# One scale per pair of input tiles, weight sums written in place, and a table for attention's pace, in a two-branch kernel

## The chip, the cores and the metric

The kernel runs on one core of a Trainium2 chip. The core's engines work side by side, each through its own instructions in order: TensorE (PE; its weight loads are shown apart as PEld), VectorE (DVE), ScalarE (ACT), GpSimd (POOL) and SyncE (SP, which here only issues DMAs). The metric is the device time of one execution in microseconds (us). The time before is 1770.59 us, the median of three runs (1760.23 to 1774.22).

## The reference

Two independent computations share one output, side by side along the last axis:

```python
# branch A: attention of 32 heads of width 32 over a sliding window of 256 keys
q, k, v = split(x @ wqkv)                      # x: 2048 x 1024
scores = q @ k.T * 32 ** -0.5, masked to 0 <= i - j < 256
a = (softmax(scores) @ v) @ wo
# branch B: a Fourier layer written with four matrices
p0 = xb @ dft_hid_re.T ; p1 = xb @ dft_hid_im.T    # 2048 x 1024
b = dft_seq_re @ p0 - dft_seq_im @ p1
out = concatenate([a, b], axis=-1)             # 2048 x 2048, float32
```

All inputs are float32. Branch A's inputs are larger by a factor of 8 than the usual draw, so its softmax is sharp and its products need more than half precision.

## The kernel before

**Products.** A float32 matrix is divided by a power of two taken from its largest entry, and split into a high and a low float16 part (`split`: ACT writes the high part, DVE the low part); a product is then three float16 passes (high-high, high-low, low-high). The largest entry is found by `top` (a DVE reduction of one tile to a column), `spread` (over the tiles), and `scale_of` (a small transposing matmul on PE, and four or five small DVE instructions). The large products of branch B and the last one of A are done in two-by-two blocks with seven multiplications in place of eight (`seven`), for which sums of blocks are made beforehand.

**Order of the work.** PE's order is written out. First come 96 *order steps* of one 128x512 product each (24 large matmuls): the q, k and v projections. Then come 48 *units* in four *rounds* of twelve, 84 large matmuls each: four units of branch B's first product (kind x: pairs of tiles of `xb` times the hidden weights, `p1_`), then eight of its second (kind c: rows of the sequence matrix, `p2_`). Rounds are numbered by p (real, imaginary part) and c (left, right half); the first round stores its result plainly, the others add to the output through an accumulating DMA of POOL (`store`). Eight last products with `wo` follow (`po`).

**Attention in between.** Attention has 256 blocks (a group of two heads by 128 queries). It is a Python generator; `tick(n)` is called after every 8 (steps) or 4 (units) large matmuls, adds `n * rate[0]` to an account, and takes one half-block from the generator for each whole number. A block's chain: PE makes scores (`s`, `far`), DVE masks them and finds maxima (`mx`), ACT exponentiates and writes the high half, DVE the low half (`hl`), SP transposes by DMA (`t<-hl`), POOL masks two copies (`z`, `t`), and six blocks later (`LAG`) PE multiplies by v (`pv<-vt`). Before, the pace is one number times a share: 0.6 in steps, 1 in units, 0.2 in a round's fourth unit. That is 0.88 blocks a step and 5.11 a unit.

**Preparation in the steps.** `at(n, f)` hangs work on step n. `scan(key, k, n, step)` loads k tiles one after the other from step n and reduces each one step later. Before: `wd1` (imaginary hidden weights) from step 9, `B` (all sixteen tiles of `xb`, for one scale) from 22, `wd0` from 40, `wo` from 73. `xp(m, n)` makes the sums of the m-th pair of `xb` tiles, eight pairs from step 41, four steps apart, and stores them to DRAM (`xs`); `wp(p, k, n)` makes the sums of the hidden weights. Both use one buffer, `wx`, for their float32 raws (`praw`) and results (`pout`). The hidden weights' seven sums live in seven slots: four in `reg2`, three in `wx`. For p = 0 the first four were written into their slots, the last three went to DRAM and came back at step 91; for p = 1 all seven go to DRAM and are loaded in the second round (`w_slot`).

**Other queues.** Without an explicit constraint, the framework's scheduler decides where in an engine's queue an instruction lands, SP's above all.

Of the kernel before, what the change touches and what calls it, by code (L numbers as in the profile page):

```python
# [53 lines left out]
def fused_kernel(ctx: ExitStack, tc: tile.TileContext, xa, wqk, wv, wo, xb, wd, cs, out):  # L54
# [7 lines left out]
    wds = [tc.dram_tile((7, P, 2, 4, CH), F16, name=f"wds{p}") for p in range(2)]  # L62
# [116 lines left out]
    vB4 = const.tile([P, 1], F32, name="vB4")  # L179
# [200 lines left out]
    def at(n, f, *args):  # L380
# [100 lines left out]
    def scan_load(key, i):  # L481
        if key == "B":
            src, shape = xb[i], [ND, P]
        elif key == "wo":
# [12 lines left out]
    def scan_scale(key):  # L497
        if key == "B":
            scale_of(key, vB[:, 0:1], vB[:, 1:2])
            nc.vector.tensor_scalar(vB4, vB[:, 1:2], 0.25, None, op0=ALU.mult)  # L500
        elif key[:2] == "wd":
# [9 lines left out]
    def fa_known():  # L511
        for p in range(2):
# [38 lines left out]
    def scan(key, k, n, step):  # L551
        for i in range(k):
            at(n + step * i, scan_load, key, i)
            at(n + step * i + 1, scan_top, key, i, k)
        at(n + step * (k - 1) + 3, scan_scale, key)
# [29 lines left out]
    def xp_step(n, m, step):  # L585
        r1, r2 = (praw(m % 2 * 2 + j).rearrange("p (d t) -> p d t", t=P) for j in range(2))

        def made(at_, src):
# [3 lines left out]
                  src, vB4, behind_act)  # L592
            keep(n + 1, xs[m][:, at_:at_ + 2 * w], t)

        if step == 0:
            made(0, r1)
        elif step == 1:
# [3 lines left out]
        elif step == 2:  # L601
# [6 lines left out]
    def wp_load(p, k):  # L608
        for b in range(4):
            nc.sync.dma_start(praw(b), wd[p, 1 - b % 2, 2 * (b // 2) + k].rearrange("p d c -> p (d c)"))  # L610

    def wp_step(n, p, k, step):
        b1, b2, b3, b4 = (praw(b).rearrange("p (d c) -> p d c", c=CH) for b in range(4))

        def fill(pos, raw):
            if p == 0 and pos < 4:
                t = reg2o[:, pos, :, 2 * k:2 * k + 2]
            else:
                t = pout().rearrange("p (h d c) -> p h d c", h=2, c=CH)
                keep(n + 1, wds[p][pos, :, :, 2 * k:2 * k + 2], t)  # L620
# [38 lines left out]
    def w_slot(p, pos):  # L659
# [520 lines left out]
```

## Time and profile before

The profiled execution took 1775.21 us, 1773.5 of them between the first and the last instruction (the span).

| | us |
|---|---|
| median of the runs | 1770.59 |
| profiled execution | 1775.21 |
| its span | 1773.5 |
| steps 0 to 39 (and the start) | 236.0 |
| steps 40 to 71 | 183.9 |
| steps 72 to 95 | 141.2 |
| units 0 to 11 (round one) | 256.7 |
| units 12 to 23 (round two) | 275.9 |
| units 24 to 35 (round three) | 281.2 |
| units 36 to 47 (round four) | 248.6 |
| the last products | 150.0 |

How to read it: a row of the windows view has a stretch and its length, then busy time of PE, PEld, DVE, ACT and POOL, each with its instructions in brackets, then the granted share of the TensorE clock, the mean busy share of the sixteen DMA engines, and GB/s. A row of waits has who waited for whom: us in total, times, the longest. A row of groups has line, engine, operation, out<-in, shapes, count, then busy us, mean ns of one, then the idle time before them and what ended it. Rows in order of time have start and length.

### The profile page before, as it was taken

Reading aid. Unit: us, or ns where it says so; the run is one execution under the profiler, and the core shown is the slowest. Engines: PE = TensorE matmul, PEld = TensorE weight load, DVE = VectorE, ACT = ScalarE, POOL = GpSimd, SP = SyncE. Lnnn points to the kernel's source line nnn. Section 1 sums busy time; section 2 is a strip of 40 time slices with the busy share of each in tenths; the row PEclk is TensorE's granted clock in tenths of the full one; section 3 lists DMA queues with packets and bytes.
Section 4 is the critical chain, followed back from the end, with each engine's and each line's share of the span. In section 5 each row is a group of like instructions: output and inputs, shape, how many; then the busy total and the mean of one; then the engine's idle time right before and its main releaser. Section 6 shows DMA issues by size and latency. Waiting matters only on the chain.

```text
span 1773.5 us, 30898 instructions
## 1 busy us (share of the span) xinstructions
PE 1710.9 (96%) x10980; PEld 854.1 (48%) x10980; DVE 1381.1 (78%) x2365; ACT 1116.0 (63%) x1939; POOL 431.5 (24%) x698
## 2 busy tenths in 40 slices
PE   9999999999999999999999989999898998999998
PEld 4444454545545545555544544545444444444443
DVE  7878987888894899985998866899686697586542
ACT  3335565665564888886878866888685686463322
POOL 0000221322132223332333423325243323100000
PEclk9999999999999999999999999999999999999999
DMA  9649999999999849999999999959989966854431
GB/s 344 199 158 281 323 283 300 286 270 310 270 253 259 198 100 210 213 209 237 194 282 172 207 163 229 206 115 186 186 171 204 205 144 105 231 99 95 131 95 72
DMA packets 473084, 363.32 MB, mean 205 GB/s; under 512 B 377440, under 2 KB 410208, under 8 KB 471648
## 3 DMA queue, kind: packets, MB, share of 16 engines
q1 hardware_dynamic: 466016, 336.17, 76.2%
q0 software_dynamic: 6912, 25.17, 8.9%
q8 instruction: 86, 1.41, 0.3%
q14 instruction: 70, 0.57, 0.1%
HBM read 178.52 MB, written 109.31 MB: 162 GB/s over the span
## 4 chain that ended last, share of the span: by engine, by line
PE 59%; DVE 18%; DMA 12%; ACT 5%; issue 4%; SPq 1%; POOL 1%; DVEq 0%; ACTq 0%; POOLq 0%
PE p_a L113 15%; PE pv L113 9%; PE p_b L113 7%; DMA t<-hl 7%; PE pq L113 7%; PE pk L113 6%; PE po_a L113 5%; PE p_c L113 4%; PE po_b L113 2%; PE s L113 2%; DVE hl L253 2%; DVE mx L239 2%; DVE reg L795 2%; DVE raw_u L752 1%; DVE y L996 1%
## 5 line engine op out<-in xcount | busy, mean ns | idle before, releaser
L249 ACT ACTIVATE s<-s,bias,escs 128x256 f32<-128x256 f32 (+1 forms) x512 | 270.1, 528 | 11.7
L253 DVE TENSOR_TENSOR hl<-s,hl 128x512 f16<-128x512 f32 (+1 forms) x256 | 170.6, 667 | 92.6 <-ACT hl L252 91.8
L113 PE MATMUL p_a<-reg,un_c 128*128 128x512 f16 x960 | 229.5, 381 | 7.7 <-ACT y L994 7.6
L267 POOL TENSOR_SCALAR_AFFINE_SELECT z<-t 128x512 f16<-128x512 f16 x224 | 171.9, 770 | 248.6 <-PE pv L113 128.2
L242 ACT ACTIVATE bias<-mx,pshift,escs 128x2 f32<-128x2 f32 x256 | 98.3, 384 | 168.2 <-DVE mx L239 165.7
L113 PEld LDWEIGHTS <-reg 128*128 128x128 f16 x1344 | 129.4, 98 | 143.0 <-issue 3.0
L246 POOL TENSOR_SCALAR mark<-bias 128x1 f32<-128x1 f32 x128 | 50.9, 398 | 570.3 <-ACT bias L242 547.3
L252 ACT ACTIVATE hl<-s 128x512 f16<-128x512 f32 (+1 forms) x256 | 148.8, 581 | 55.2 <-DMA t<-hl 49.8
L269 POOL TENSOR_SCALAR_AFFINE_SELECT t<-t 128x512 f16<-128x512 f16 x224 | 174.3, 783 | 12.4
L113 PE MATMUL pk<-reg,wu_k 128*128 128x512 f16 x768 | 174.6, 381 | 2.7 <-DVE wu_k L120 2.7
L113 PEld LDWEIGHTS <-un_b 128*128 128x128 f16 x1152 | 110.0, 98 | 132.7 <-issue 12.6
L239 DVE TENSOR_REDUCE mx<-s 128x2 f32<-128x512 f32 (+1 forms) x256 | 171.0, 668 | 2.9
L113 PE MATMUL pv<-reg,reg 128*128 128x512 f16 x768 | 171.9, 379 | 0.0
L113 PEld LDWEIGHTS <-un_c 128*128 128x128 f16 x1152 | 110.0, 98 | 127.3 <-issue 12.3
L113 PEld LDWEIGHTS <-un_a 128*128 128x128 f16 x1152 | 110.2, 98 | 121.5 <-issue 7.1
L113 PE MATMUL pq<-reg,wu_q 128*128 128x512 f16 x672 | 150.0, 379 | 3.8 <-DVE yq L120 2.9
L113 PE MATMUL p_b<-reg,un_b 128*128 128x512 f16 x576 | 139.7, 382 | 11.9 <-DVE reg L795 4.9
L113 PE MATMUL p_a<-reg,un_a 128*128 128x512 f16 x576 | 138.4, 382 | 3.4 <-DVE y L996 3.4
L113 PE MATMUL p_c<-reg,un_a 128*128 128x512 f16 x576 | 136.5, 379 | 0.0
L113 PEld LDWEIGHTS <-qk 96*128 96x128 f16 x1056 | 88.3, 98 | 79.8 <-issue 10.6
L237 DVE COPY_PREDICATED s<-upper,far 128x256 f32<-128x256 uint32 x224 | 94.4, 421 | 35.7 <-PE s L113 35.4
L113 PEld LDWEIGHTS <-wu_k 128*128 128x128 f16 x768 | 74.5, 98 | 85.4 <-DVE wu_k L120 3.2
(196 smaller groups left out, 3076.4 us busy)
## 6 DMA issues: line engine op xcount, KB each, us to landing
raw_u<-in_cs_dram SPq DMA_DIRECT2D x64, 512.0 KB, 4.9
qk<-qk SPq DMA_DIRECT2D x64, 384.0 KB, 5.3
out_dram<-y POOLq DMA_DIRECT2D x36, 512.0 KB, 8.0
qk<-yq SPq DMA_DIRECT2D x96, 128.0 KB, 4.2
qk<-yk SPq DMA_DIRECT2D x96, 128.0 KB, 3.7
xs<-wx SPq DMA_DIRECT2D x24, 512.0 KB, 5.0
wds<-wx SPq DMA_DIRECT2D x20, 512.0 KB, 5.7
vs<-yv SPq DMA_DIRECT2D x32, 264.0 KB, 4.4
```

Of the source, the lines that this page charges most:

```text
L113: fixed[:] = [nc.tensor.matmul(*args, **kwargs)]
L237: nc.vector.copy_predicated(s[:, :, P:], upper2, d["far"] if nb == 3 else never2)
L239: nc.vector.tensor_reduce(mx, sv, axis=AX.X, op=ALU.max, negate=True)
L242: nc.scalar.activation(bias, mx, AF.Identity, bias=pshift, scale=es)
L246: marks[:] = [nc.gpsimd.tensor_scalar(mark, bias[:, 0:1], 1.0, None, op0=ALU.mult)]
L249: nc.scalar.activation(sv[:, h], sv[:, h], AF.Exp, bias=bias[:, h:h + 1], scale=es)
L252: nc.scalar.activation(hi, sv, AF.Copy)
L253: behind[:] = [nc.vector.tensor_tensor(lo, sv, hi, op=ALU.subtract)]
L267: nc.gpsimd.affine_select(out=z, in_=pk, compare_op=ALU.is_gt, fill=0.0, base=0, pattern=[[0, 4], [-1, P]], channel_multiplier=1)
L269: nc.gpsimd.affine_select(out=pk, in_=pk, compare_op=ALU.is_ge, fill=0.0, base=0, pattern=[[0, 4], [1, P]], channel_multiplier=-1)
L752: nc.vector.tensor_tensor(o, a, b, op=op)
L795: nc.vector.tensor_tensor(lo, src, hi, op=ALU.subtract)
```

## The change

Three things change.

1. *A scale per pair.* The scan `B` goes. Each `xp(m)` loads its pair a step earlier, reduces its two tiles (`top_xp`), and takes a scale of its own (`vxp`), so it runs over six steps in place of four. Part one's eviction multiplies by a column that evens the pairs' scales (`fx`). `wo` is now scanned at steps 20 to 38, `wd0` from 42.
2. *Part-one sums in place.* For p = 0 the raws of the hidden weights come into the rotating pool of five (`load_raw`) in place of `wx`, and all seven sums are written into their slots; the stores and loads between go. For p = 1 the seven loads are hung on other turns of the second round. `w_finish` of the q and k weights runs three steps ahead of their use, not two.
3. *Pace.* A table in blocks per unit, for the x units (`FIRST`) and c units (`SECOND`) of each round; the rest is spread over steps 24 to 95 by `EARLY`.

```diff
-    wds = [tc.dram_tile((7, P, 2, 4, CH), F16, name=f"wds{p}") for p in range(2)]
+    wds = tc.dram_tile((7, P, 2, 4, CH), F16, name="wds")
...
-    SHARE = {"p": 0.6, "x": (1.0, 1.0, 1.0, 0.2), "c": 1.0}
-    base = 2.0 * (NG * NCH * 2 * QB + 2 * LAG) / (
-        24 * (len(order) - START) * SHARE["p"] + 84 * (4 * sum(SHARE["x"]) + (24 + LAST - 0.7) * SHARE["c"]))
-    rate = [base * SHARE["p"]]
+    FIRST = ((7.2, 5.2, 4.9, 0.6), (5.2, 5.2, 4.9, 0.6), (3.3, 5.2, 4.9, 0.6), (3.3, 5.2, 4.9, 0.6))
+    SECOND = ((2.4, 5.0, 5.0, 5.0, 5.0, 5.0, 5.0, 7.0), (2.2, 4.6, 4.6, 4.6, 4.6, 3.9, 3.9, 4.2),
+              (2.4, 4.6, 4.6, 4.6, 4.6, 5.0, 5.0, 4.2), (2.4, 4.6, 4.6, 4.6))
+    EARLY = {n: (0.9, 1.05, 1.05, 1.0, 0.95, 1.05)[(n - START) // 12] for n in range(START, len(order))}
+    in_units = sum(sum(a) for a in FIRST + SECOND) - 0.7 * SECOND[3][LAST - 1]
+    early = (NG * NCH * 2 * QB + LAG - in_units) / sum(EARLY.values())
+    rate = [0.0]
...
     def fa_known():
+        nc.vector.tensor_reduce(vB[:, 0:1], vxp[:, 0], axis=AX.X, op=ALU.max)
+        nc.vector.reciprocal(vB[:, 1:2], vB[:, 0:1])
+        nc.vector.tensor_scalar(fx, vxp[:, 0], vB[:, 1:2], 4.0 * DOWN, op0=ALU.mult, op1=ALU.mult)
...
-            at(n - 2, w_finish, kd, g)
+            at(n - 3, w_finish, kd, g)
...
     scan("wd1", 8, 9, 1)
-    scan("B", 16, 22, 1)
-    scan("wd0", 8, 40, 4)
-    scan("wo", 8, 73, 2)
-    at(72, fa_known)
+    scan("wo", 8, 20, 2.5)
+    scan("wd0", 8, 42, 3.5)
+    at(75, fa_known)
...
         if step == 0:
+            for j, r in enumerate((r1, r2)):
+                top(f"xp{m}", r, j, 2)
+            spread(f"xp{m}", 2)
+        elif step == 1:
+            scale_of(f"xp{m}", vxp[:, 0, m:m + 1], vxp[:, 1, m:m + 1])
+            nc.vector.tensor_scalar(vxp[:, 1, m:m + 1], vxp[:, 1, m:m + 1], 0.25, None, op0=ALU.mult)
             made(0, r1)
...
-            nc.sync.dma_start(praw(b), wd[p, 1 - b % 2, 2 * (b // 2) + k].rearrange("p d c -> p (d c)"))
+            src = wd[p, 1 - b % 2, 2 * (b // 2) + k]
+            if p == 1:
+                nc.sync.dma_start(praw(b), src.rearrange("p d c -> p (d c)"))
+            else:
+                held[k, b] = load_raw(src, [2, CH], f"wd{k}_{b}")
...
-            if p == 0 and pos < 4:
-                t = reg2o[:, pos, :, 2 * k:2 * k + 2]
+            if p == 0:
+                t = slot(pos)[:, :, 2 * k:2 * k + 2]
...
-        at(n - 1, xp_load, m)
-        for step in range(4):
-            at(n + step, xp_step, n + step, m, step)
+        at(n - 2, xp_load, m)
+        for i, step in enumerate((0, 2, 3, 4, 5)):
+            at(n - 1 + step, xp_step, n - 1 + step, m, i)
...
-    for pos in range(4, 7):
-        at(91, w_slot, 0, pos)
...
+            rate[0] = 2 * early * EARLY.get(n, 0.85) / 24
...
-                for pos in range(7):
-                    do(c0 + pos, 2, w_slot, 1, pos)
+                for pos, (j, turn) in enumerate(((0, 1), (0, 4), (4, 2), (5, 2), (5, 5), (6, 2), (6, 5))):
+                    do(c0 + j, turn, w_slot, pos)
...
-            rate[0] = base * (SHARE["x"][i] if kind == "x" else SHARE["c"])
+            rate[0] = 2 * ((FIRST if kind == "x" else SECOND)[2 * p + c] + (0,) * 8)[i] / 84
...
-                seven(f"p1_{n}", i, uns.pop(n), slot, y1, y2, 4.0 * DOWN, lambda t, y: None, x_hook)
+                seven(f"p1_{n}", i, uns.pop(n), slot, y1, y2, fx[:, 4 * c + i:4 * c + i + 1],
+                      lambda t, y: None, x_hook)
```

Where the pace puts the blocks, counted in PE's order (blocks begun when the step or unit begins):

| | step 40 | step 72 | step 96, unit 0 | unit 12 | unit 24 | unit 36 |
|---|---|---|---|---|---|---|
| before | 15 | 43 | 64 | 121 | 178 | 236 |
| changed | 17 | 54 | 81 | 138 | 187 | 236 |

DVE's order around the second pair of `xb` tiles, near step 46. Here `wx` holds the pair's raws and results, `yk` is an evicted projection, `s`, `mx` and `hl` belong to attention blocks. Before:

```order
L237 COPY_PREDICATED s_2570<-upper,far 128x2x128
L752 TENSOR_TENSOR wx<-wx 128x512
L239 TENSOR_REDUCE mx_2576<-s_2570 128x2
L752 TENSOR_TENSOR wx<-wx 128x512
L120 SCALAR_TENSOR_TENSOR yk_1_2606<-pk_1_2561,kf,yk_1_2606 128x512
L120 SCALAR_TENSOR_TENSOR wx<-wx,vB_105 128x512
L237 COPY_PREDICATED s_2626<-upper,far 128x2x128
```

The same engine and place in the changed kernel:

```order
L120 SCALAR_TENSOR_TENSOR yk_3_2593<-pk_3_2545,kf,yk_3_2593 128x512
L120 TENSOR_REDUCE top_xp_2606<-wx 128x1 x2
L120 SCALAR_TENSOR_TENSOR wx<-wx,vxp 128x1024
L238 COPY_PREDICATED s_2621<-upper,far 128x2x128
L317 TENSOR_TENSOR ohl_0_3_2525<-o_0_3_2367,ohl_0_3_2525 128x256
L254 TENSOR_TENSOR hl_2568<-s_2554,hl_2568 128x512
L120 TENSOR_REDUCE top_xp_2609<-top_xp_2606 128x1
L240 TENSOR_REDUCE mx_2627<-s_2621 128x2
L120 SCALAR_TENSOR_TENSOR yk_0_2694<-pk_0_2612,kf,yk_0_2694 128x512
```

The pair's two reductions (`top_xp`, both in one row) and the small instructions of its scale now stand among the evictions and score maxima of these steps, and read the tile that a DMA has just filled.

SP's order at the start of the second round's c units, with the seven loads of the imaginary weights' sums (`<-wds`), the sequence matrix's tiles (`raw_u`) and attention's transposes. Before:

```order
L660 DMA reg_85<-wds_62 128x4096 x3
L255 DMA_TRANSPOSE t_10620<-hl_10617 128x8x128
L660 DMA reg_85<-wds_62 128x4096
L318 DMA_TRANSPOSE ot_0_0_10717<-ohl_0_0_10714 128x4x128
L660 DMA wx<-wds_62 128x4096
L105 DMA raw_u_0_10812<-in_cs_dram 128x1024
L205 DMA qk_0_3_10852<-qk 96x2048
L660 DMA wx<-wds_62 128x4096
L105 DMA raw_u_1_10933<-in_cs_dram 128x1024
L337 DMA ots<-ot_0_0_10717 128x512
L660 DMA wx<-wds_62 128x4096
```

The same queue and place in the changed kernel:

```order
L671 DMA reg_84<-wds 128x4096
L319 DMA_TRANSPOSE ot_1_0_11254<-ohl_1_0_11251 128x4x128
L671 DMA reg_84<-wds 128x4096
L256 DMA_TRANSPOSE t_11299<-hl_11296 128x8x128
L338 DMA ots<-ot_1_0_11254 128x512
L671 DMA reg_84<-wds 128x4096 x2
L671 DMA wx<-wds 128x4096 x2
L105 DMA raw_u_0_11440<-in_cs_dram 128x1024
L105 DMA raw_u_1_11557<-in_cs_dram 128x1024
L671 DMA wx<-wds 128x4096
```

The seven loads stand together at the head of the c units in both; the turns on which the code hangs them reach over seven units.

More of the change, by code (lines that the diff above doesn't have):

```diff
@@ L178, in fused_kernel @@
     vB = vs_of("B")
-    vB4 = const.tile([P, 1], F32, name="vB4")
+    vxp = const.tile([P, 2, 8], F32, name="vxp")
+    fx = const.tile([P, 8], F32, name="fx")
     vwd = const.tile([P, 2, 2], F32, name="vwd")
@@ L481, in scan_load @@
     def scan_load(key, i):
-        if key == "B":
-            src, shape = xb[i], [ND, P]
-        elif key == "wo":
+        if key == "wo":
             src, shape = wo[i // 4, i % 4], [2, CH]
@@ L600, in xp_step @@
             sub(r2[:, :4], r2[:, :4], r2[:, 4:], ALU.add)
-        elif step == 2:
+        elif step == 3:
             sub(r2[:, 4:], r2[:, 4:], r1[:, :4])
@@ L609, in wp_load @@
         for b in range(4):
[L610 removed]
+            src = wd[p, 1 - b % 2, 2 * (b // 2) + k]
[3 more added lines that the diff above has]
+                held[k, b] = load_raw(src, [2, CH], f"wd{k}_{b}")
     def wp_step(n, p, k, step):
[L613 removed]
+        b1, b2, b3, b4 = (praw(b).rearrange("p (d c) -> p d c", c=CH) if p else held[k, b] for b in range(4))
         def fill(pos, raw):
[L616 to L617 removed]
+            if p == 0:
+                t = slot(pos)[:, :, 2 * k:2 * k + 2]
             else:
                 t = pout().rearrange("p (h d c) -> p h d c", h=2, c=CH)
[L620 removed]
+                keep(n + 1, wds[pos, :, :, 2 * k:2 * k + 2], t)
             split(t[:, 0], t[:, 1], raw, vwd[:, p, 1:2], behind_act)
```

19 lines of the change are left out of this document (8 added, 11 removed).

## The prediction

> **What bounds the kernel now.** I read the page's first part, then the windows by stage (cut where the 24 matmuls of an order step, or the 84 of a unit, begin), then who waited for whom.
>
> ```profile
> PE 1710.9 (96%) x10980; PEld 854.1 (48%) x10980; DVE 1381.1 (78%) x2365; ACT 1116.0 (63%) x1939; POOL 431.5 (24%) x698
> ...
> 236.00:419.90 183.90, 183.80 (x1202) 92.39 (x1200) 153.83 (x262) 110.77 (x187) 44.88 (x91) 1.00 1.06 287
> 419.90:561.10 141.20, 138.32 (x905) 69.64 (x902) 112.07 (x190) 78.71 (x134) 33.66 (x48) 1.00 1.01 274
> 561.10:817.80 256.70, 254.48 (x1900) 133.99 (x1898) 223.30 (x418) 208.54 (x390) 84.74 (x129) 1.00 0.84 190
> 817.80:1093.70 275.90, 260.38 (x1890) 134.97 (x1889) 224.22 (x417) 207.05 (x390) 95.48 (x144) 0.98 1.03 208
> 1093.70:1374.90 281.20, 260.87 (x1904) 135.65 (x1902) 225.91 (x419) 210.01 (x391) 97.97 (x144) 0.98 0.94 183
> 1374.90:1623.50 248.60, 237.36 (x1401) 114.51 (x1400) 187.78 (x302) 158.49 (x253) 53.93 (x72) 0.98 0.70 150
> ```
>
> PE is busy 1710.9 of 1773.5 us, so only 62.6 us of gaps can be won, with what the clock loses around them. The first row is steps 40 to 71 of the ordered part; PE has no gap there and DVE sits idle 30 us. Rows three to five are three rounds of the same twelve units with 57, 57 and 58 attention blocks: 256.7, 275.9 and 281.2 us. Rounds two and three thus lose 19.2 and 24.5 us against round one. The waits say to what:
>
> ```profile
> PE far L113 <- DVE s L237: 8.8, 3, 5.4
> PE p_a L113 <- ACT y L994: 8.2, 4, 7.1
> PE far L113 <- DMA qk<-qk: 7.2, 2, 5.7
> PE pv L113 <- POOL z L267: 6.9, 2, 5.9
> ...
> PE p_b L113 <- DVE reg L795: 4.9, 3, 2.0
> ...
> PE pk L113 <- DVE wu_k L120: 2.7, 1, 2.7
> ```
>
> The four on top are few and long, and belong to the attention chain. The longest but two, seen in order of time on SP's queue and on PE:
>
> ```profile
> 1029.10 8.36 SPq L255 DMA_TRANSPOSE t<-hl  x1
> 1037.55 0.74 SPq L205 DMA_DIRECT2D qk<-qk  x1
> ...
> 1043.76 0.29 PE L113 MATMUL far<-qk,qk 96*128 96x128 f16 x1 [5.73 <-DMA qk<-qk]
> ```
>
> SP issues in order. A transpose of a block's weights held it for 8.36 us, the next q/k load was issued behind it, and PE stood 5.73 us. Such waits fall where the DMA share is 1.03 and 0.94; round one, at 0.84 with as many blocks, has none.
>
> **The change part by part.**
>
> *Pace.* Counted in PE's order, by step 40 there are 17 blocks begun (15 before), by step 72 54 (43), by step 96 81 (64), at the second round 138 (121), the third 187 (178), the fourth 236 (236). So 9 blocks come into steps 40 to 71, and 8 and 9 leave rounds two and three. PE's own work on a block only moves; its price is needed for one stage. Twelve large matmuls of the chain take 2.59 us, 0.216 each:
>
> ```profile
> 1509.31 2.59 PE p_a L113 x12
> ...
> L113 PE MATMUL pk<-reg,wu_k 128*128 128x512 f16 x768 | 174.6, 381 | 2.7 <-DVE wu_k L120 2.7
> L166 PE MATMUL pt_u<-ident,top_u 128*128 128x128 f32 x32 | 8.8, 274 | 0.4 <-DVE o L301 0.4
> ```
>
> In steps 40 to 71, 768 of them are 165.8 us; the rest of the 183.9 us, 18.1 us, went to 28 blocks: 0.65 us each. The eight new small transposes cost 0.155 us each, as a row's 381 ns stand for 216 and theirs say 274: 1.2 us. Changed, PE needs 165.8 + 37 × 0.65 + 1.2 = 191.0 us.
>
> *DVE in that stage.* Durations and, in the last two rows, how closely instructions follow:
>
> ```profile
> L120 DVE TENSOR_REDUCE top_B<-raw_B 128x1 f32<-128x1024 f32 x16 | 19.3, 1209 | 0.0
> L239 DVE TENSOR_REDUCE mx<-s 128x2 f32<-128x512 f32 x240 | 164.4, 685 | 2.7
> L253 DVE TENSOR_TENSOR hl<-s,hl 128x512 f16<-128x512 f32 x240 | 164.1, 684 | 92.3 <-ACT hl L252 91.6
> L237 DVE COPY_PREDICATED s<-upper,far 128x256 f32<-128x256 uint32 x224 | 94.4, 421 | 35.7 <-PE s L113 35.4
> L301 DVE TENSOR_REDUCE o<-pv 128x132 f32<-128x264 f32 x128 | 54.4, 425 | 23.4 <-PE pv L113 23.0
> L316 DVE TENSOR_TENSOR ohl<-o,ohl 128x256 f16<-128x256 f32 x64 | 29.2, 457 | 2.3 <-ACT ohl L315 2.3
> L312 DVE TENSOR_TENSOR o<-o,rs 128x256 f32<-128x256 f32 x64 | 29.2, 456 | 1.0
> L310 DVE RECIPROCAL rs<-o 128x8 f32<-128x8 f32 x64 | 12.7, 198 | 1.0
> L120 DVE TENSOR_REDUCE sc_u<-pt_u 128x1 f32<-128x128 f32 x32 | 9.1, 286 | 5.3 <-PE pt_u L166 5.3
> L120 DVE TENSOR_SCALAR sc_u<-sc_u 128x1 f32<-128x1 f32 x32 | 4.8, 150 | 0.7
> ...
> 1028.85 0.68 DVE L239 TENSOR_REDUCE mx<-s 128x2 f32<-128x512 f32 x1
> 1029.45 0.68 DVE L752 TENSOR_TENSOR raw_u<-raw_u,raw_u 128x512 f32<-128x512 f32 x1
> ```
>
> Back to back, 0.68 us costs 0.60: I take 0.08 off each. The sixteen reductions of the old search stood in steps 22 to 38; sixteen of the same shape now stand in 40 to 71: 16 × 1.13 = 18.1 us. Eight scales of six small instructions, 0.286 + 5 × 0.15 − 6 × 0.08 = 0.56 us: 4.5 us. A block costs 0.685 + 0.684 + 0.421 + 0.425/2 + (0.457 + 0.456 + 0.198)/4 = 2.28 us, less 4.25 × 0.08: 1.94; nine are 17.5 us. Together 40.1, and DVE's 153.8 becomes 193.9 against PE's 191.0. The scan of the hidden weights stays in the stage. So PE's cover there is gone: **DVE becomes the bound by a little**. Bounds: nothing, if three product banks and three score tiles ride it out; or 33 us, if DVE keeps all its 30.1 us of idle time (224.0 − 191.0). DVE has worked a stretch with next to no idle time and no PE gap:
>
> ```profile
> 489.10:511.90 22.80, 22.80 (x149) 11.44 (x147) 22.34 (x33) 13.89 (x23) 7.12 (x8) 1.00 0.88 225
> ```
>
> It is the row nearest to the new load; at its 98%, 193.9 needs 197.9: **+6.9**. The transposes are **+1.2**. The following stage has 29 us of DVE idle; six blocks more (+11.6) and eight reductions of the output weights fewer (−9.0, now at steps 20 to 38) change nothing.
>
> By the Trainium skill, page "SBUF — State Buffer", section "SBUF: two separate sides", a GpSimd instruction and a DVE one with two SBUF inputs exclude each other for a whole instruction, which speaks against more selects (two a block on POOL) beside a full DVE. The trace shows the same instruction at 762 ns among attention and 692 ns after it:
>
> ```profile
> L752 DVE TENSOR_TENSOR raw_u<-raw_u,raw_u 128x512 f32<-128x512 f32 x96 | 73.1, 762 | 0.6
> L752 DVE TENSOR_TENSOR r<-r,r 128x512 f32<-128x512 f32 x24 | 16.6, 692 | 0.8
> ```
>
> By these rows eighteen more selects cost DVE at most 18 × 0.07 = 1.3 us; by the rule in full, up to 18 selects' length. I leave it in the range.
>
> *Loads.* Sixteen 512 KB loads of the old search leave SP's queue at steps 22 to 38, and eight of the output weights take their place; nothing on PE's path waited for them: 0.
>
> *Weight sums in place.* The diff drops six stores of 512 KB and three 1 MB loads at step 91; the raws go to the rotating pool, whose five buffers are free again when its weight loads need them, as each raw's last reader stands at least a step ahead of the reuse. Nothing on PE's path: 0. Their finish one step earlier (three ahead of use, not two) takes the `wu_k` wait at step 36: **−2.7**.
>
> *Starts of rounds.* The first second-part unit of a round now has 2 blocks, not 4, beside its late sums, where DVE was full:
>
> ```profile
> 902.10:925.70 23.60, 21.53 (x155) 11.22 (x155) 23.23 (x44) 18.60 (x35) 9.14 (x10) 1.00 0.89 267
> ```
>
> That takes the three `reg` waits, 1.6 each; those of rounds two and three are inside the 19.2 and 24.5. Round one: **−1.6**.
>
> *Rounds two and three.* The seven 1 MB loads given other turns are not spread: SP's order has them in ten rows now, in eleven before. What helps is the pace. Without attention the share was 0.52:
>
> ```profile
> 1550.00:1600.00 50.00, 49.16 (x228) 22.17 (x227) 42.61 (x55) 34.40 (x44) 3.68 (x5) 1.00 0.52 100
> ```
>
> So attention made some 0.51 and 0.42 of the 1.03 and 0.94; 8 of 57 and 9 of 58 blocks fewer take 0.07 off each. That is 37% of the way to round one's 0.84 for round two and 65% for round three: **−7.1** and **−15.9**. Bounds: nothing (a chain that is late by its own latency stays late) and all 43.7. In the fourth round the tail's blocks stand thinner; of its 5.9 us wait on `z` and some 1 us that the clock lost with it I take half: **−3.5**, between 0 and −7.
>
> Sum: −2.7 − 1.6 − 7.1 − 15.9 − 3.5 + 6.9 + 1.2 = −22.7 us. The profiled execution took 1775.2 us and would take 1752.5; the median of the runs is 4.6 below it, and off 1770.6 the same is **1748 us**.
>
> Page "TensorE: Matmul & The Clock Gate" of the Trainium skill, Part 1, has the matmul clock halved after an idle window of some 3.4 us. The 0.98 of the rounds with long waits and 1.00 elsewhere agree; the loss is inside the stage differences, and many short DVE waits would not be charged so.
>
> **The rivals.**
> - *All long waits go* (round one shows the same blocks without any) and DVE rides through: −2.7 − 1.6 − 43.7 − 7 + 1.2 = −53.8: 1717 us.
> - *The pace was not the cause*: transposes stay late because accumulating output stores of POOL share the engines, and by the last units of each round blocks are as dense as before. Terms of rounds two to four fall away: −2.7 − 1.6 + 6.9 + 1.2 = +3.8, 1774 us. The new turns of the loads that spread nothing belong here: a part that doesn't do what it says.
> - *Slower: DVE's search waits for its loads.* A pair is now searched on DVE one step after its two loads are issued; DVE is in order, and score maxima and evictions queue behind it, which PE waits for. DVE has waited so:
>
> ```profile
> L752 DVE TENSOR_TENSOR wx<-wx 128x1024 f32<-128x1024 f32 x16 | 20.6, 1287 | 7.6 <-DMA wx<-in_wd_dram 7.6
> ```
>
> That is 7.6 us over four groups of loads, 1.9 each, 15.2 us for eight pairs. (193.9 + 15.2)/0.98 = 213.4, 22.4 over PE's need; if the slow stage also brings no relief later, −2.7 − 1.6 + 22.4 + 1.2 = +19.3: 1790 us. It decides as soon as DVE's work and waits in steps 40 to 71 pass 191 us, which the sum above already does by 3; against it stands that the old search read its loads one step after issue with 0.0 idle time (the `top_B` row).
>
> **How the numbers follow.** One per cent is 17.7 us, about what a measurement of this kernel can tell from no change: below 1752.9 is faster, above 1788.3 slower. The forecast, with the relief of rounds two and three between 10 and 35 us, has 0.50 (1736 to 1762), of which 0.33 lies below 1752.9 since its middle does. All waits gone: 0.20. Pace not the cause: 0.17, within 1%. DVE waiting for loads: 0.13. Faster 0.53, within 1% 0.34, slower 0.13. The range goes from the second case's 1717 to 1784, which leaves out the slow case and takes in the forecast with DVE's upper bound (−22.7 − 6.9 + 33 = +3.4, 1774).
>
> **What would show it.** In the profile after: steps 40 to 71 last 195 to 200 us with DVE busy over 185 (if PE has no gap there, the 6.9 is wrong; if they pass 205, the slow rival holds, and PE's waits there name DVE); no wait of `pk` on `wu_k` over 1 us; no `reg` wait over 1 us at a round's start; rounds two and three at 255 to 270 us each, about 6 of the fall being work that moved, with a DMA share under 1.0; at most two attention waits over 4 us (still four or more: the pace was not the cause). I am wrong outright if a new long wait appears where the pace rose, in the first unit of round one (7.2 blocks against 5.1), where six blocks of lag are 6 × (84 × 0.216 + 7.2 × 0.65)/7.2 = 19 us.

## The result, and the profile after

The changed kernel takes **1749.8 us** (median of ten runs, 1740.3 to 1752.9) beside 1770.0 us for the kernel before in the same runs: a ratio of 0.9884, with a 95% interval of 0.9859 to 0.9909. The prediction was 1748 us. Its profiled execution took 1749.9 us with a span of 1748.2. Some executions of a version take over 1.5% longer than its fastest; ratios leave these out, and no stage length is read from one.

The page's first part, then the windows by stage, of the changed kernel (columns as in the tables of before):

```profile
PE 1705.0 (98%) x10987; PEld 853.1 (49%) x10987; DVE 1387.7 (79%) x2410; ACT 1119.9 (64%) x1939; POOL 423.0 (24%) x698
```

```profile
234.50:436.80 202.30, 192.48 (x1342) 99.00 (x1341) 189.97 (x369) 125.47 (x220) 53.95 (x108) 0.99 1.05 276
436.80:583.90 147.10, 143.68 (x1005) 73.75 (x1004) 115.03 (x199) 92.76 (x162) 42.66 (x65) 0.99 0.85 217
583.90:839.80 255.90, 254.04 (x1885) 133.64 (x1881) 224.80 (x417) 206.25 (x385) 77.34 (x124) 1.00 0.84 189
839.80:1097.10 257.30, 251.88 (x1760) 129.20 (x1759) 210.68 (x384) 196.37 (x357) 85.13 (x128) 0.99 1.03 214
1097.10:1359.10 262.00, 253.63 (x1783) 130.30 (x1782) 208.81 (x382) 194.31 (x355) 87.50 (x125) 0.99 0.88 180
1359.10:1598.50 239.40, 234.31 (x1402) 113.69 (x1401) 188.14 (x301) 158.05 (x253) 50.09 (x72) 1.00 0.71 154
```

PE's busy time hardly fell (1710.9 to 1705.0) while the span lost 25.3 us: gaps went. In the first row (steps 40 to 71) the change loses 18.4 us, in the second (steps 72 to 95) 5.9; in rounds two, three and four (rows four to six) it wins 18.6, 19.2 and 9.2. The DMA share of round two stays at 1.03 although most of its loss is gone.

Who waited for whom, PE's first rows in the changed kernel:

```profile
PE far L113 <- DVE s L238: 5.2, 4, 2.9
PE pt_u L166 <- DVE top_u L120: 4.7, 1, 4.7
PE pk L113 <- DVE yk L120: 4.3, 1, 4.3
PE pq L113 <- DVE yq L120: 3.8, 2, 3.4
PE p_a L113 <- ACT y L1003: 3.6, 2, 3.0
...
PE p_b L113 <- DVE reg L803: 2.1, 2, 1.4
```

Of the attention chain's long waits of before (5.4, 7.1, 5.7 and 5.9 us) none of these is left. Two long ones stand on evictions in the ordered steps, `yk` and `yq`, at places where PE had not waited before. The longest, 4.7 us for `pt_u` (the scale of a tile of the sequence matrix), falls in round three. Some 20 us earlier, SP and POOL show this:

```profile
1221.81 14.24 SPq L256 DMA_TRANSPOSE t<-hl  x3
...
1222.18 0.92 POOL L1078 DMA_DIRECT2D out_dram<-y  x1 [0.26 <-DVE sc_u L120]
```

Three transposes held SP for 14.24 us while POOL issued two accumulating stores (at 1222.2 and 1223.4 us), which took 14.6 and 15.7 us to land. ACT stood 6.8 us until a transpose had landed, DVE 6.75 us for ACT, and PE for DVE. So one wait of the old kind is there.

### The profile page after: what moved, and what is told of

Read it like the earlier page. It is cut to its first block, busy times and chain, and to the rows that moved or that the text cites. A ratio compares the mean times of both kernels' runs of the same rounds, so it can differ in the third digit from the quotient of the medians.

```text
span 1748.2 us, 30996 instructions
## 1 busy us (share of the span) xinstructions
PE 1705.0 (98%) x10987; PEld 853.1 (49%) x10987; DVE 1387.7 (79%) x2410; ACT 1119.9 (64%) x1939; POOL 423.0 (24%) x698
## 4 chain that ended last, share of the span: by engine, by line
PE 62%; DVE 18%; DMA 7%; ACT 6%; issue 6%; SPq 1%; POOL 1%; DVEq 0%; ACTq 0%; POOLq 0%
PE p_a L113 17%; PE p_b L113 8%; PE pv L113 7%; PE pk L113 7%; PE pq L113 7%; PE po_a L113 5%; PE p_c L113 4%; DMA t<-hl 3%; PE po_b L113 2%; PE s L113 2%; DVE reg L803 2%; DVE mx L240 2%; DVE hl L254 1%; ACT s L250 1%; DVE s L238 1%
## 5 line engine op out<-in xcount | busy, mean ns | idle before, releaser
L250 ACT ACTIVATE s<-s,bias,escs 128x256 f32<-128x256 f32 (+1 forms) x512 | 269.8, 528 | 11.3
L268 POOL TENSOR_SCALAR_AFFINE_SELECT z<-t 128x512 f16<-128x512 f16 x224 | 163.3, 735 | 261.7 <-PE pv L113 183.5
L243 ACT ACTIVATE bias<-mx,pshift,escs 128x2 f32<-128x2 f32 x256 | 98.2, 384 | 149.9 <-DVE mx L240 145.1
L247 POOL TENSOR_SCALAR mark<-bias 128x1 f32<-128x1 f32 x128 | 46.9, 366 | 577.6 <-ACT bias L243 574.6
L270 POOL TENSOR_SCALAR_AFFINE_SELECT t<-t 128x512 f16<-128x512 f16 x224 | 178.0, 802 | 11.9
L238 DVE COPY_PREDICATED s<-upper,far 128x256 f32<-128x256 uint32 x224 | 94.3, 421 | 38.6 <-PE s L113 37.2
```

The costliest lines, as they stand in the source:

```text
L238: nc.vector.copy_predicated(s[:, :, P:], upper2, d["far"] if nb == 3 else never2)
L243: nc.scalar.activation(bias, mx, AF.Identity, bias=pshift, scale=es)
L247: marks[:] = [nc.gpsimd.tensor_scalar(mark, bias[:, 0:1], 1.0, None, op0=ALU.mult)]
L250: nc.scalar.activation(sv[:, h], sv[:, h], AF.Exp, bias=bias[:, h:h + 1], scale=es)
L268: nc.gpsimd.affine_select(out=z, in_=pk, compare_op=ALU.is_gt, fill=0.0, base=0, pattern=[[0, 4], [-1, P]], channel_multiplier=1)
L270: nc.gpsimd.affine_select(out=pk, in_=pk, compare_op=ALU.is_ge, fill=0.0, base=0, pattern=[[0, 4], [1, P]], channel_multiplier=-1)
```

## The experiments

The table has the stage lengths in us of each profiled execution, cut as in the windows above, and each kernel's ratio to the kernel before with its 95% interval. Of the run without the new pace only the times are used. A row is one execution: the six other versions with adding stores and 49 blocks in each of rounds two and three took 509.7 to 521.8 us for the two together, so differences of a few us between single rows there mean little.

| kernel | steps 24–39 | 40–71 | 72–95 | round 1 | 2 | 3 | 4 | ratio (interval) |
|---|---|---|---|---|---|---|---|---|
| before | 95.5 | 183.9 | 141.2 | 256.7 | 275.9 | 281.2 | 248.6 | 1 |
| changed | 94.0 | 202.3 | 147.1 | 255.9 | 257.3 | 262.0 | 239.4 | 0.9884 (0.9859–0.9909) |
| pace alone | 98.3 | 211.7 | 150.8 | 259.6 | 261.5 | 260.3 | 241.0 | 1.0021 (0.9988–1.0053) |
| scale alone | 90.8 | 192.0 | 144.5 | 256.3 | 272.2 | 275.9 | 250.8 | 1.0038 (1.0000–1.0076) |
| all but pace | | | | | | | | 0.9978 (0.9935–1.0020) |
| all but sums in place | 96.9 | 210.1 | 149.2 | 255.9 | 253.4 | 256.3 | 240.5 | 0.9960 (0.9923–0.9998) |
| even pace | 96.8 | 205.1 | 148.7 | 257.7 | 267.7 | 260.6 | 247.5 | 1.0012 (0.9984–1.0041) |
| thin starts | 98.1 | 183.8 | 145.5 | 256.9 | 280.7 | 272.3 | 250.1 | 1.0059 (1.0025–1.0094) |
| no searches | 93.8 | 212.0 | 146.1 | 254.7 | 254.6 | 255.7 | 242.5 | 0.9922 (0.9886–0.9958) |
| one load | 94.8 | 205.4 | 145.4 | 254.8 | 256.4 | 264.3 | 241.4 | 0.9926 (0.9891–0.9961) |
| fewer blocks in 40–71 | 94.3 | 203.1 | 150.5 | 258.5 | 257.7 | 257.0 | 245.4 | 0.9939 (0.9904–0.9975) |
| subtraction held | 93.8 | 197.7 | 142.0 | 255.4 | 256.4 | 258.7 | 243.0 | 0.9842 (0.9791–0.9894) |
| before, plain stores | 95.3 | 183.6 | 145.1 | 256.9 | 256.1 | 259.0 | 242.0 | 0.9783 (0.9704–0.9862) |
| changed, plain stores | 94.7 | 201.6 | 146.3 | 254.6 | 252.5 | 252.1 | 237.6 | 0.9830 (0.9799–0.9861) |

### Which part does it

*Pace alone*: the kernel before with only the new table (`FIRST`, `SECOND`, `EARLY`) in place of `SHARE`.

> The kernel before with the new pace table alone. Two accounts of where the 25 us came from. Theory: the pace did it, in rounds two to four; the search of the pairs only cost time in steps 40 to 71, together with the nine blocks moved there. Then rounds two and three last 519 us together, within 8, as in the changed kernel (557 before), steps 40 to 71 last 189 to 194 us (PE's need is 189.8, DVE's 171) against 202 in the changed kernel, and the whole is 1735 to 1745 us, below the changed kernel. Rival: the relief needs the lighter DMA load of the other two edits too. Then rounds two and three stay over 535 us and the whole is 1755 to 1768 us.

*Scale alone*: the kernel before with only the scale per pair.

```diff
-                  src, vB4, behind_act)
+                  src, vxp[:, 1, m:m + 1], behind_act)
...
-    scan("B", 16, 22, 1)
```

> The kernel before with the scale per pair alone: no search of all sixteen tiles at steps 22 to 38, a search per pair at 40 to 71; old pace, old scans of the two weights, old places of the sums. Theory (DVE is overfull only with search and pace together): DVE's 153.8 us in steps 40 to 71 become 176 of a PE need of 185.1, so the stage lasts 184 to 188 us, rounds two and three stay at 557 within 10, and the whole is 1766 to 1775 us. Rival (a search that stands in order before evictions makes PE wait even on a DVE that has room): the stage lasts 192 to 202 us as in the changed kernel, and the whole is 1778 to 1790 us.

*All but pace*: the changed kernel with `SHARE` back.

> The changed kernel with the old pace: the two other edits together. The pace alone has just given nothing (its rounds two and three lasted 522 us, but steps 40 to 71 took 212), and the scale per pair alone nothing. Theory (the parts help one another: the pace empties the rounds, the other edits make room on the DMA engines for the blocks that it moves into the steps): without the pace rounds two and three are back at 545 to 560 us, steps 40 to 71 at 184 to 193, and the whole is 1755 to 1768 us. Rival (the gain is the other two edits' own, and the pace is a bystander): 1745 to 1752 us with rounds two and three under 530.

*All but sums in place*: the changed kernel with the part-one raws in `wx`, the stores and loads of three sums, and `w_finish` two steps ahead again.

```diff
-            at(n - 3, w_finish, kd, g)
+            at(n - 2, w_finish, kd, g)
...
-                held[k, b] = load_raw(src, [2, CH], f"wd{k}_{b}")
+            nc.sync.dma_start(praw(b), wd[p, 1 - b % 2, 2 * (b // 2) + k].rearrange("p d c -> p (d c)"))
```

> The changed kernel without its second part: the part-one weight sums go to DRAM and are loaded back as before, their raws through the tile that the second input's pairs hold; scale per pair and pace stay. Theory H: no subtraction of weights waits near step 69, so steps 40-71 at 195 to 199 us; steps 72-95 at 148 to 153 us for the added stores and loads (147.2 in the changed kernel); the total 1745 to 1752 us. Theory D: steps 40-71 at 201 to 203 us, total 1750 to 1756 us. If the parts only help together (pace alone and scale alone gave nothing each), the total shows whether the in-place sums are needed for that: 1765 us or more if they are.

Pace alone: 1768.0 us; scale alone: 1771.4; all but pace: 1768.7; all but the in-place sums: 1757.3. **Neither the pace nor the scale is worth anything alone**; the sums in place were not run alone. Pace and scale together win 0.4%, and the third part as much again and more; the pace, added to the other two, wins some 0.9% (0.9978 to 0.9884).

The table shows the bargain. The new pace wins 14.4 and 20.9 us in rounds two and three also when alone, and then pays 27.8 us in steps 40 to 71 and 9.6 in steps 72 to 95. With the other parts it pays 18.4 and 5.9.

So pace alone shortened the rounds as its theory had it, but took 211.7 us in steps 40 to 71 where 189 to 194 was expected, and its total fell to the rival. Scale alone took 192.0 us there, where its rival began (192 to 202), while its total fell to the theory. The run without the in-place sums missed both of its theories: 210.1 us, where 195 to 203 was expected, and a total above both, though short of the 1765 us that would have shown the in-place sums to be needed.

### Why rounds two and three shorten

*Even pace*: the kernel before with 0.844 for 0.6 as the steps' share. That begins 80 blocks before the units, with 53 and 52 in rounds two and three, evenly spread. *Thin starts*: the kernel before with a table that keeps the old totals (58 and 56 blocks in rounds two and three), but gives each round's first c unit 2.2 to 2.4 blocks.

```diff
-    SHARE = {"p": 0.6, "x": (1.0, 1.0, 1.0, 0.2), "c": 1.0}
+    SHARE = {"p": 0.844, "x": (1.0, 1.0, 1.0, 0.2), "c": 1.0}
```

> The kernel before with one number changed: the share of the steps is 0.844, not 0.6, so a uniform pace of 4.66 blocks a unit, 80 blocks before the units (81 in the changed kernel), and 53 and 52 blocks in rounds two and three (57 and 58 before, 49 and 49 changed); the starts of rounds are not thinned. Theory A (the number of blocks in a round makes the long waits): each block fewer took about 1.5 us of waiting between before and after, so rounds two and three lose 13 and 16 us beyond their work, and last 266 and 269 us. Theory B (the thin start of each round did it): they lose 19 and 24 as before and last 273 and 277 us, only the moved work being gone. Steps 40 to 71 last 188 to 192 us under both. The whole: 1750 to 1758 by A, 1765 to 1772 by B.

> The kernel before with the new kind of table, but the old number of blocks per round (62 before the units, 58 and 56 in rounds two and three): only the first c unit of each round is thinned to about 2 blocks, and the other units carry 5.3. Theory A (the number of blocks): rounds two and three last 275 and 278 us, as before, and the whole is 1764 to 1774 us. Theory B (the thin start): the losses fall to those of the changed kernel, 7 and 11 us, so rounds two and three last 264 and 266 us and the whole is 1742 to 1752 us.

1768.7 us with the even pace, 1776.2 with the thin starts. By the rounds it is the number of blocks and not where a round is thin. The even pace's total fell to theory B all the same, because steps 40 to 71 took 205.1 us, where both theories had 188 to 192; the thin starts were slower than either theory said. What is lost in rounds two and three together, against round one of before (256.7 us for 57 blocks, each block more or less at the prediction's 0.65 us): 43.1 us before (57 and 58 blocks), 39.6 with thin starts (58 and 56), 20.7 with the even pace (53 and 52), 16.3 in the changed kernel (49 and 49). The other versions with 49 and 49 blocks and adding stores lose between 6.7 and 18.8 us, so the last figure is good to some 10 us.

*Before, plain stores*: why should round one run 57 blocks with no loss and round two not? One thing that differs is the store: round one's results are stored plainly, on SP's queue, those of the later rounds are added to DRAM by POOL. The run makes POOL's stores plain (the parts of the sum are then not added up, so the result is wrong).

```diff
-                nc.gpsimd.dma_start(dst, src, accum_op=ALU.add)
+                nc.gpsimd.dma_start(dst, src)
```

> The kernel before, with the stores of rounds two to four that add to the result in DRAM made plain stores: the parts of the sum are not added up, and nothing else differs. If these stores hold the queues that rounds two and three wait for: rounds two and three at 255 to 262 us each (275.9 and 281.2 before), total 1735 to 1750 us. If the waits there come from attention's number of blocks, as the runs with the new pace say: 272 to 282 us each, total within 5 us of before.

1729.3 us. Rounds two and three take 256.1 and 259.0 us with all their 57 and 58 blocks: of 43.1 us, 1.1 are left. POOL's DMA queue from 817 to 1375 us of each execution, which are rounds two and three of the kernel before (packets, MB, share of sixteen engines' time), first in the kernel before, then with plain stores, then in the changed kernel:

```profile
q0 software_dynamic: 4320, 15.73, 18.1%
```

```profile
q0 software_dynamic: 4608, 16.78, 9.4%
```

```profile
q0 software_dynamic: 4608, 16.78, 18.4%
```

Over those 557 us, by these shares, an adding store of 512 KB takes 0.181 × 557 / 30 = 3.4 us of all sixteen engines, a plain one 0.094 × 557 / 32 = 1.6 us. What it does to attention shows in the transposes on SP's queue (shortest, median, longest in ns) and in how long POOL's masks waited for them (us in total, times); before, and with plain stores:

```profile
L255 SPq DMA_TRANSPOSE t<-hl x256: 1188/1276/8357, 151.3 to 1485.9; - x128
...
  POOL z L267: 120.3, 38
```

```profile
L255 SPq DMA_TRANSPOSE t<-hl x256: 1188/1247/4169, 151.0 to 1446.4; - x128
...
  POOL z L267: 47.7, 27
```

The transpose of 8.36 us in the prediction's rows was issued at 1029.1 us, 6.7 us after POOL had issued two adding stores:

```profile
1022.40 1.82 POOL L1069 DMA_DIRECT2D out_dram<-y  x2 [0.26 <-DVE fu L732]
```

*Changed, plain stores*: the same edit on the changed kernel (again nothing is added up), to see whether pace and stores are one loss or two.

> The changed kernel with the stores that add to the result in DRAM made plain stores: the parts of the sum are not added up. Theory Q (attention's blocks and the adding stores press on the same queues, so that the new pace and the plain stores are two ways out of one loss): the plain stores add little to the changed kernel, rounds two and three stay at 250 to 256 us (257.3 and 262.0 with the adding stores, 256.1 and 259.0 in the kernel before with plain stores), and the whole comes to 1735 to 1745 us, which is 6 to 16 us longer than the kernel before with plain stores: the sign of the change turns, since what it costs in the steps is no longer paid back. Theory R (two losses apart from each other): rounds two to four shorten by another 15 us or more, total below 1730 us, and the change still gains.

1733.1 us. Rounds two and three come to 252.5 and 252.1 us, of which 251.5 are what 49 blocks need; all but 1.6 of the 16.3 us that the changed kernel still lost are gone as well. So it is one loss: the adding stores make it where attention is dense; fewer blocks take away some 27 of its 43.1 us, plain stores nearly all. On the total neither theory hit: above the 1730 of the one, 2 us short of the other's 1735. With plain stores the change is worth nothing that can be measured (ratios 0.9783 and 0.9830 to before, intervals overlapping); it still pays 18 us in steps 40 to 71.

### What the ordered steps pay

*No searches*: the changed kernel with the searches and scales of pairs one to seven left out (they take the first pair's scale). *One load*: seven of the eight loads of the `wd0` scan left out, its reductions reading a constant tile. *Fewer blocks in 40–71*: `EARLY` changed so that five blocks fewer begin in steps 40 to 71 and five more in steps 72 to 95.

```diff
-                top(f"xp{m}", r, j, 2)
+                if m == 0:
+                    top(f"xp{m}", r, j, 2)
```

```diff
+        if key == "wd0" and i:
+            seen[key, i] = ident.unsqueeze(1).to_broadcast([P, ND, P])
+            return
```

```diff
-    EARLY = {n: (0.9, 1.05, 1.05, 1.0, 0.95, 1.05)[(n - START) // 12] for n in range(START, len(order))}
+    EARLY = {n: (0.9, 1.0, 0.92, 0.83, 1.17, 1.18)[(n - START) // 12] for n in range(START, len(order))}
```

> The changed kernel with the search and scale of pairs 1 to 7 left out (they take pair 0's scale): DVE has 14 reductions and 42 small instructions less in steps 40 to 71, some 19 us, and no DMA changes. Theory DVE (DVE's order and load set that stage, as the prediction had it): it falls from 202 us to 190 to 194. Theory DMA (the stage is long because nine more blocks' transposes and loads meet DMA engines that were already at a share of 1.06): it stays at 197 to 203 us.

> The changed kernel with seven of the eight loads of the scan of the real hidden weights left out (3.7 MB of the 56 MB in steps 40 to 71); in their place the same reductions read a tile that lies in SBUF, so DVE has the same work. Theory DMA: at 276 GB/s 3.7 MB are 13 us, and steps 40 to 71 fall from 202 us to 190 to 196. Theory DVE: no change there, 199 to 204.

> The changed kernel with one line changed: the steps' table is 0.9, 1.0, 0.92, 0.83, 1.17, 1.18, so that 32 blocks, not 37, fall into steps 40 to 71, and 32, not 27, into steps 72 to 95, where DVE idles 32 us and the DMA share is 0.85. Both theories expect less waiting in steps 40 to 71: 188 to 194 us, not 202, of which 3.3 are work that moved. Steps 72 to 95 take 150 to 153 us. The whole: 1738 to 1747 us, below the changed kernel; if the moved blocks wait as long in the later stage, 1748 to 1753.

1755.7, 1754.8 and 1757.7 us: none is faster than the changed kernel, and none shortens steps 40 to 71. No searches took 212.0 us there and missed both theories; one load took 205.4, nearest to theory DVE; fewer blocks took 203.1, where both theories had 188 to 194. The window of that stage with no searches:

```profile
234.40:446.40 212.00, 195.05 (x1334) 98.84 (x1333) 177.02 (x318) 126.30 (x221) 53.10 (x107) 0.97 1.04 266
```

DVE has 13 us less to do there (177.0 against 190.0) and the stage is 9.7 us *longer*. So the sum of DVE's work alone doesn't set it. In order of time DVE shows what else does. The changed kernel, on DVE and then on PE, around both new waits:

```profile
414.02 0.43 DVE L238 COPY_PREDICATED s<-upper,far 128x256 f32<-128x256 uint32 x1
415.95 1.23 DVE L760 TENSOR_TENSOR raw_wd<-raw_wd,raw_wd 128x1024 f32<-128x1024 f32 x1 [1.50 <-DMA raw_wd<-in_wd_dram]
417.09 0.15 DVE L120 TENSOR_REDUCE top_xp<-top_xp 128x1 f32<-128x2 f32 x1
417.15 0.74 DVE L120 SCALAR_TENSOR_TENSOR yk<-pk,kf,yk 128x512 f16<-128x512 f32 x1
...
497.49 1.23 DVE L760 TENSOR_TENSOR raw_wd<-raw_wd,raw_wd 128x1024 f32<-128x1024 f32 x1 [7.75 <-DMA raw_wd<-in_wd_dram]
498.63 0.28 DVE L120 TENSOR_REDUCE scw<-pt_wk 128x1 f32<-128x128 f32 x1
498.83 0.68 DVE L120 SCALAR_TENSOR_TENSOR yq<-pq,yq 128x512 f16<-128x512 f32 x1
...
417.95 5.10 PE L113 MATMUL pk<-reg,wu_k 128*128 128x512 f16 x16 [4.32 <-DVE yk L120]
...
499.57 5.25 PE L113 MATMUL pq<-reg,wu_q 128*128 128x512 f16 x16 [3.42 <-DVE yq L120]
```

The first subtraction of each group of part-one weight sums (`raw_wd`, hung on steps 75 and 83) stands ahead of evictions in DVE's order and waits there for its load, 1.50 and 7.75 us; behind it stand `yk` and `yq`, for which PE waits. The kernel defines `sub` twice, under one name: the first, next to the weight sums, binds the subtraction behind the last eviction; the second, meant for the sequence matrix, binds it to nothing and replaces the first, as the row's line (L760) shows. So the scheduler put the first subtraction some six steps ahead of its turn. Both kernels have this. Without the searches the same instruction waited 3.03 us and PE 8.44 us:

```profile
423.39 1.23 DVE L765 TENSOR_TENSOR raw_wd<-raw_wd,raw_wd 128x1024 f32<-128x1024 f32 x1 [3.03 <-DMA raw_wd<-in_wd_dram]
...
426.59 4.00 PE L113 MATMUL pk<-reg,wu_k 128*128 128x512 f16 x9 [8.44 <-DVE yk L120]
```

The same two subtractions wait in the other versions as well. Here they are in the kernel before, where PE waits behind neither; with pace alone, with the PE wait that follows the first; and with all but the in-place sums:

```profile
407.30 1.24 DVE L752 TENSOR_TENSOR wx<-wx 128x1024 f32<-128x1024 f32 x1 [1.08 <-DMA wx<-in_wd_dram]
477.63 1.23 DVE L752 TENSOR_TENSOR wx<-wx 128x1024 f32<-128x1024 f32 x1 [3.39 <-DMA wx<-in_wd_dram]
```

```profile
434.39 1.23 DVE L755 TENSOR_TENSOR wx<-wx 128x1024 f32<-128x1024 f32 x1 [5.68 <-DMA wx<-in_wd_dram]
515.14 1.22 DVE L755 TENSOR_TENSOR wx<-wx 128x1024 f32<-128x1024 f32 x1 [6.71 <-DMA wx<-in_wd_dram]
...
437.28 0.26 PE L113 MATMUL far<-qk,qk 96*128 96x128 f16 x1 [5.71 <-DVE s L237]
```

```profile
441.19 1.23 DVE L759 TENSOR_TENSOR wx<-wx 128x1024 f32<-128x1024 f32 x1 [4.17 <-DMA wx<-in_wd_dram]
510.69 1.23 DVE L759 TENSOR_TENSOR wx<-wx 128x1024 f32<-128x1024 f32 x1 [7.23 <-DMA wx<-in_wd_dram]
```

*Subtraction held*: the changed kernel, with that one instruction of each group bound behind the last eviction. In the program's order the first moves from row 591 to row 669 of DVE.

```diff
             fill(0, b1)
-            sub(b2, b2, b1)
+            with tc.issue_after(behind[0].ins) if p == 0 else nullcontext():
+                sub(b2, b2, b1)
```

> The changed kernel with one VectorE instruction held back: the first subtraction of the part-one weight sums (raw_wd_1 <- raw_wd_1, raw_wd_0) may not stand ahead of the step's evictions any more, and moves from the 591st to the 669th row of VectorE's order. Theory H (that subtraction waits for its load with the evictions queued behind it): no TensorE wait over 3 us at 400 to 430 us from the start, steps 40-71 at 196 to 199 us (202.2 in the changed kernel), the total 3 to 6 us below the changed kernel, 1743 to 1747 us. Theory D (VectorE has too much to do there): VectorE's work in steps 40-71 is the same but for one subtraction of 1.2 us, so 200 to 203 us there and no difference in the total. Theory L (the loads contend): 202 us too, with the long wait on another instruction.

**1740.5 us** (six runs, 1732.9 to 1745.9), the fastest version that does the whole work: 0.9842 of the kernel before. Its interval overlaps the changed kernel's at the edge; the medians, measured apart, lie 9 us from each other, more than the 3 to 6 us that were expected. Its windows of steps 40 to 71 and 72 to 95, PE's longest waits in the first, and DVE's rows where the subtraction stood:

```profile
235.00:432.70 197.70, 190.96 (x1342) 98.52 (x1340) 188.57 (x364) 125.02 (x220) 52.66 (x107) 1.00 1.05 280
432.70:574.70 142.00, 142.00 (x1007) 73.46 (x1006) 116.59 (x202) 92.48 (x162) 41.27 (x65) 1.00 0.93 230
```

```profile
PE far L113 <- DVE s L238: 3.8, 3, 2.9
PE pk L113 <- DVE yk L120: 1.6, 1, 1.6
PE far L113 <- DVE top_xp L120: 1.2, 1, 1.2
```

```profile
414.19 0.42 DVE L238 COPY_PREDICATED s<-upper,far 128x256 f32<-128x256 uint32 x1
414.53 0.15 DVE L120 TENSOR_REDUCE top_xp<-top_xp 128x1 f32<-128x2 f32 x1
414.59 0.74 DVE L120 SCALAR_TENSOR_TENSOR yk<-pk,kf,yk 128x512 f16<-128x512 f32 x1
```

The first stage became 4.6 us shorter, as expected with the subtraction as the cause; the second became 5.1 us shorter and has no PE gap at all. The eviction `yk` starts 2.6 us earlier than in the changed kernel, and PE's wait for it fell from 4.32 to 1.58 us. That a single moved instruction does this, with DVE's work (188.6 against 190.0) and the DMA share (1.05) as before, settles it for these two waits: the changed kernel with plain stores, which is the same up to round one, repeats the two stages within 1 us (201.6 and 146.3).

In the version without the in-place sums no PE wait over 1.3 us follows the first subtraction within steps 40 to 71. Its stage is long for other waits: 4.7 us for a `yk` at the start, 2.8 for a pair's scale, 2.2 for a pair's search, 1.7 for a weight's scale. The first began with ACT waiting 7.5 us for a store of `yk` to land; what held that store is open.

## Why the prediction was right or wrong

The total is right, 1748 against 1749.8, and so is the sign of every stage but steps 72 to 95. On the profiled execution the forecast was −22.7 us and came out as −25.3. That it came so near is in part luck: the relief of rounds two and four was sized too small by some 12 us, and so was the price of the steps by 6; round three and round one went some 3 us the other way.

- **Steps 24 to 39, −2.7**: the stage lost 1.4 us with two blocks (1.3 us) more in it, which is −2.7, and no `wu_k` wait is left. The cause I named isn't shown: with `w_finish` back at two steps ahead that wait is absent too. Scale alone, where it also stands at two, takes the stage to 90.8 us with PE busy throughout; so what left with the old search, which I priced at 0, is the likelier cause.
- **Steps 40 to 71, +6.9 and +1.2**: the stage took 202.3 us against PE's need of 191.0, a loss of 11.3, not 6.9. PE's need was right: 190.96 us busy once the held subtraction ends the long wait. The step that failed is the one after: *"DVE becomes the bound by a little ... at its 98%"*. DVE's work came to 190.0 us, not 193.9; and DVE at 177.0 us of work lost more, not less, so neither its sum nor the 98% rule carries the term. The 6.7 us that stay with the subtraction held (197.7) sit close to 6.9, which is luck: they are three kinds of short waits in DVE's order. The rest is the subtraction that the scheduler put ahead of the evictions.
- **Weight sums in place, 0**: I wrote "nothing on PE's path", yet their first subtraction stands on it: it waits ahead of evictions, and that costs some 9.7 us in the two stages (4.6 + 5.1). The edit didn't bring this wait. With the old places of the sums and the new pace it is there as well (5.68 and 6.71 us), and in the kernel before (1.08 and 3.39 us) PE didn't feel it; what uncovers it is the fuller steps. The sums in place win 0.8% on top of the other two parts (0.9960 to 0.9884). Why isn't shown; they and the scale per pair spare traffic (363.3 to 348.6 MB), which is one candidate.
- **Steps 72 to 95, "change nothing"**: +5.9, of which six blocks of PE work are 3.9. The 3.4 us wait for `yq` comes from the second such subtraction; against it, a wait of 2.5 us for another `yq`, which the kernel before had there, is gone.
- **The slower rival** had the right mechanism at the wrong place. DVE's order does wait for a load with evictions behind it, but the pairs' searches don't wait: in no version did one stand idle for its load. In the changed kernel no wait of PE over 1.2 us names `top_xp` (up to 2.2 and 4.4 us in two others, where the searches stand ahead of evictions), while the row that I quoted to price them (7.6 us for `wx<-in_wd_dram`) was the weight sums' own subtraction. That it was covered before by DVE's idle time was no reason that it would be after.
- **Round one, −1.6**: −0.8. No new long wait in its first unit. One `reg` wait of 1.4 us is left, in round two, where I had said none over 1.
- **Rounds two and three, −7.1 and −15.9**: beyond the work that moved (5.2 and 5.9 us) they lost 13.4 and 13.3 us less than before. Together 26.7 against 23.0, and wrongly shared out, since I scaled by the DMA share: round two's share is still 1.03 (predicted under 1.0) with its long waits gone. The mechanism was half right. Fewer blocks take the waits away, by their number; but what made the waits was the adding stores, which I had as a rival in which the pace would *not* help. Both are true at once: plain stores take 42 of the 43 us, and the pace 27 of the same 43.
- **Round four, −3.5**: −9.2 with as many blocks, beyond my bound of −7; the 5.9 us wait on `z` went whole, and the stage's clock rose from 0.98 to 1.00. Versions with this pace and adding stores took 239.4 to 245.4 us here, so part of the 9.2 is chance.
- **The new turns of the seven loads** spread nothing, as said.

The clock's part shows in single rows. Sixteen matmuls of `pk` took 5.10 us after PE had stood 4.32 us, and 3.61 us in this row of the version with the subtraction held, after 1.58:

```profile
415.38 3.61 PE L113 MATMUL pk<-reg,wu_k 128*128 128x512 f16 x16 [1.58 <-DVE yk L120]
```

The waits of 4.32 and 3.42 us thus cost about 1.5 us each on top of themselves. By the Trainium skill, page "TensorE: Matmul & The Clock Gate", Part 1, the clock halves after an idle window of about 3.4 us. These traces agree in part (sixteen matmuls took 5.25 us after 3.42, and nothing was added after 1.58): in the kernel before it also fell after a wait of 2.69 us (fourteen took 4.83 us), and in the changed kernel it held after one of 2.89 us (twenty-one took 4.70 us), so the length of the wait alone doesn't decide.

## What to carry to other kernels

A stage's sum of busy times says whether an engine can keep up, not what stalls it: look in order of time for the instruction that stands ahead of the evictions and waits for a load, and bind it behind them. A wait that an engine's idle time covers today comes to light when that engine gets more work. When work is moved out of a crowded stage, ask what makes that stage crowded at all; here the kind of store weighed more than the move. Parts of a change that win nothing alone can win together: two of the three parts here were worth nothing by themselves, and all three win 1%.

## What the runs showed that I had not expected

An adding store of 512 KB took twice the DMA engine time of a plain one (3.4 against 1.6 us of all sixteen engines), and SP's longest DMA transpose took 8.4 us in the kernel before, against 4.2 with plain stores. Making them plain, in rounds two to four, takes 41 us off the kernel before, twice what the change wins. How to add the parts without such stores, and at what price, wasn't tried.
